# Tuning three places of an attention-plus-MLP kernel: the last output block in two parts, one group's key decay on another engine, and fewer load issues in one stretch

## The chip, the cores and the metric

The kernel runs on one core of a Trainium2 chip. The metric is the device time of one execution in microseconds (us). The kernel before took 225.02 us (median of 3 runs, 224.54 to 225.32).

## The reference

A block-wise linear attention with a decay per head, whose output feeds a two-layer MLP with a Mish gate:

```python
# q, k, v: (4 batches, 8 heads, 768 tokens, 64); lam: one decay per head; block = 64
for b in range(nb):
    intra = einsum('bhic,bhjc->bhij', qb, kb) * Dmask      # lam ** (i - j), lower triangle
    intra = einsum('bhij,bhjd->bhid', intra, vb)
    inter = einsum('bhid,bhde->bhie', qb * lam_pow, kv_state)
    out[:, :, sl] = intra + inter
    kv_state = lam_block * kv_state + einsum('bhsd,bhse->bhde', kb * rev_pow, vb)
x = out.transpose(0, 2, 1, 3).reshape(3072, 512)
h = x @ w_in                                               # 512 x 2048
return (h * tanh(softplus(h))) @ w_out                     # Mish; 2048 x 512
```

## The kernel before

The 768 tokens are cut into six groups (n = 0 to 5) of 128 tokens in each of the four batches; i = 4n + b numbers one batch of one group. While TensorE does the MLP of group n (16 units `ph` of the first layer, then 16 quarter-units `po` of the second), the attention of group n + 1 is slipped in between in small pieces. The queues: GpSimd issues the loads (they convert to 16 bits; only the first two of k and `lam` come through SP), SyncE (SP) the transposes, ScalarE (ACT) the outputs.

```python
    def scale_k(i):                                   # the decay of k
        t = work.tile([128, H, D], F16, name="ktil", tag="ktil", bufs=6)
        (nc.vector if i <= B else nc.gpsimd).tensor_tensor(
            out=t, in0=kn[i], in1=bc(lk, 2, D), op=ALU.mult)
        ktil[i] = t

    def turn(i):                                      # decay, then q and k transposed by DMA
        scale_k(i)
        for src, name, to in ((qn, "qraw", qraw), (ktil, "kraw", kraw)):
            to[i] = work.tile([128, JP, C], F16, name=name, tag=name, bufs=4)
            nc.sync.dma_start_transpose(out=to[i], in_=src[i].rearrange("p h c -> p (h c)"))

    ahead = [                                         # the loads of the third group
        (lambda f=f, i=i: f(i)) for i in range(2 * B, 3 * B) for f in (load_k, load_q, load_v)
    ]

    def att_a(s):                                     # first piece of one half (hf) of one batch
        ...
        if n >= NT:                                   # groups 2 to 5: k and q come transposed
            ...
            if hf == 0 and i + 2 < s.loaded:
                turn(i + 2)
            ...
            return
        ...                                           # groups 0 and 1: transposed on TensorE (pk, pq)
        if n > 0:
            if hf == 0 and i + 1 < s.loaded:
                scale_k(i + 1)
            elif hf == 0:
                turn(i + 1)
            att_w(s)                                  # state update; raw on VectorE, w on GpSimd
            ahead.pop(0)()                            # one load issue in each half

    def mm2_unit(n, b, part):
        w = NKI // WS
        if part == 0:
            po_t[0] = ps.tile([128, DMO], F32, name="po", tag="po", bufs=2)
        po = po_t[0]
        for kk in range(w):
            ...                                       # nc.tensor.matmul(po, hsg[n]..., wout[part]...)
        if part == WS - 1:
            osb = work.tile([128, DMO], F32, name="osb", tag="osb", bufs=3)
            nc.scalar.activation(osb, po, AF.Copy)
            r0 = b * S + n * C
            nc.scalar.dma_start(out=out[r0 : r0 + C, :], in_=osb)
```

The names used below: `ktil` is the decayed k, `pk` its transpose by TensorE, `kraw` its transpose by DMA; `raw` and `w` carry the attention's state, `sb` its masked scores; `hsg` is the Mish of `ph`; `osb` is the copy of the result `po` out of PSUM (TensorE's output memory), which the output DMA sends. A DMA lands when its completion is reported.

In the unit loop of group n, `turn((n + 1) * B)` and `turn((n + 1) * B + 1)` are called after the first `ph` unit (for n > 1); what is left in `ahead` is issued after the loop of n = 0.

## Time and profile before

| | before |
|---|---|
| span of the profiled run | 223.3 us |
| TensorE (PE) busy | 210.9 us, 94% |
| VectorE / ScalarE / GpSimd busy | 48% / 48% / 51% |
| PE's waits for GpSimd's `ktil`, 43 to 52 us | 0.37 + 0.54 + 0.58 us |
| PE's wait for `hsg`, 159.3 to 160.6 us | 1.29 us |
| last matmul's end to the end of the span | 4.4 us |

The page's first lines give the span and each engine's busy time; the rows of digits cut the span into 40 slices and give the busy share of each in tenths. In the views PE is TensorE, PEld its weight loads, DVE VectorE, ACT ScalarE and POOL GpSimd; a q after the name (ACTq) marks what the engine's instruction queue does, such as sending off a DMA.

```profile
span 223.3 us, 3697 instructions
...
PE 210.9 (94%) x1413; PEld 112.4 (50%) x1413; DVE 106.4 (48%) x223; ACT 106.8 (48%) x211; POOL 112.9 (51%) x139
...
PE   7697999998999999999999999999799999999992
```

TensorE is busy nearly all the time after the first four slices (22 us); only its gaps can be won. The view of waits, for PE alone, says who ended them (total us, times, longest us):

```profile
PE ph L343 <- ACT hsg L355: 1.8, 2, 1.3
PE pk L254 <- POOL ktil L181: 1.5, 3, 0.6
```

The first gap is in the second group's attention. In the timeline a row is start, duration, engine, line, operation, with idle time and releaser in brackets. PE's rows of the three waits, and the first `ph` after that stretch:

```profile
43.38 0.28 PE L254 MATMUL pk<-ident,ktil 128*128 128x128 f16 x2 [0.37 <-POOL ktil L181]
...
47.60 0.28 PE L254 MATMUL pk<-ident,ktil 128*128 128x128 f16 x2 [0.54 <-POOL ktil L181]
...
51.87 0.28 PE L254 MATMUL pk<-ident,ktil 128*128 128x128 f16 x2 [0.58 <-POOL ktil L181]
...
58.08 1.24 PE L343 MATMUL ph<-xt,win_77 128*128 128x512 f16 x5
```

GpSimd's rows of one batch in the same timeline show why: one decay, two `w`, two load issues, back to back, 4.27 us from one `ktil` to the next (50.76 - 46.49).

```profile
46.49 1.05 POOL L181 TENSOR_TENSOR ktil<-kn,lk 128x512 f16<-128x512 f16 x1
...
47.50 0.73 POOL L220 TENSOR_TENSOR w_200<-raw,lbm 128x256 f16<-128x256 f32 x1
...
48.17 0.94 POOL L77 DMA_DIRECT2D vz_69<-in_v_dram  x1
...
49.13 0.74 POOL L220 TENSOR_TENSOR w_202<-raw,lbm 128x256 f16<-128x256 f32 x1
...
49.80 0.94 POOL L70 DMA_DIRECT2D kn<-in_k_dram  x1
...
50.76 1.05 POOL L181 TENSOR_TENSOR ktil<-kn,lk 128x512 f16<-128x512 f16 x1
```

The second gap is at 159.3 us. The chain of waits, in order of time (start, length, what), runs back from PE through a Mish on ScalarE and an output DMA's issue to the landing of a transpose that has nothing to do with either:

```profile
155.18 4.32 DMA kraw<-ktil
159.49 0.02 issue
159.52 0.02 ACTq L374
...
159.57 0.35 ACTq L374
159.92 0.05 issue
159.97 0.60 ACT hsg L355
160.57 0.04 issue
160.61 6.20 PE ph L343 x28
```

ScalarE's timeline of the same moment: `osb` was ready at 157.63 + 0.60 = 158.23, the DMA that sends it went out at 159.57.

```profile
157.63 0.60 ACT L372 ACTIVATE osb<-po 128x512 f32<-128x512 f32 x1 [1.34 <-PE po L366]
159.57 0.35 ACTq L374 DMA_DIRECT2D out_dram<-osb  x1
```

Meanwhile four decays run on GpSimd, and a VectorE multiply that takes 0.41 to 0.58 us in 29 of its 32 uses takes 3.31 (the other two long ones, 1.50 and 1.32 us at 88.7 and 121.0 us, also ran beside decays on GpSimd):

```profile
154.07 4.26 POOL L181 TENSOR_TENSOR ktil<-kn,lk 128x512 f16<-128x512 f16 x4
154.12 3.31 DVE L239 TENSOR_TENSOR qT<-qraw,lq 128x256 f16<-128x256 f16 x1
```

The third gap is the tail. After these rows only the landing and the closing of the program follow, up to 223.3:

```profile
217.87 1.03 PE L366 MATMUL po<-wout_84,hsg 128*128 128x512 f16 x4
...
218.93 0.60 ACT L372 ACTIVATE osb<-po 128x512 f32<-128x512 f32 x1 [2.86 <-PE po L366]
219.56 0.34 ACTq L374 DMA_DIRECT2D out_dram<-osb  x1
```

### The profile page before, as it was taken

What the parts mean: (1) busy time and instruction counts of PE and PEld (TensorE: products, weight loads), DVE (VectorE), ACT (ScalarE), POOL (GpSimd) and SP (SyncE); (2) the same over time, 40 slices, a digit from 0 to 9 for tenths busy, and PEclk for the clock granted to TensorE, in tenths of its full rate; (3) what the DMA queues carried; (4) which work ended last, traced back from release to release, by engine and by line L of the source; (5) the groups of instructions that cost most, each with busy time, mean ns of one, the idle gap of its engine ahead of it and who ended that gap; (6) DMA issues with size and microseconds to landing.
All of it is one profiled execution on the core that took longest, in us unless ns stands there. A gap on an engine that the chain in (4) does not pass through costs nothing.

```text
span 223.3 us, 3697 instructions
## 1 busy us (share of the span) xinstructions
PE 210.9 (94%) x1413; PEld 112.4 (50%) x1413; DVE 106.4 (48%) x223; ACT 106.8 (48%) x211; POOL 112.9 (51%) x139
## 2 busy tenths in 40 slices
PE   7697999998999999999999999999799999999992
PEld 2374544565445555445555455555345555444440
DVE  7794411566409996249965059956405342000000
ACT  5984662566566322566332566323375323566121
POOL 7993344999947888339869038869300000000000
PEclk9999999999999999999999999999999999999999
DMA  6999999999994999919998919999940012100121
GB/s 108 142 152 207 204 206 171 183 143 137 146 139 50 127 141 146 199 24 105 100 152 98 182 29 114 116 154 82 190 80 0 0 65 79 47 0 3 47 94 49
DMA packets 100130, 24.62 MB, mean 110 GB/s; under 512 B 92945, under 2 KB 97041, under 8 KB 100113
## 3 DMA queue, kind: packets, MB, share of 16 engines
q0 software_dynamic: 77024, 13.37, 76.6%
q1 hardware_dynamic: 19632, 4.73, 14.5%
q10 hardware_dynamic: 3456, 6.29, 8.5%
q8 instruction: 11, 0.18, 0.3%
q14 instruction: 7, 0.05, 0.1%
HBM read 27.27 MB, written 6.29 MB: 150 GB/s over the span
## 4 chain that ended last, share of the span: by engine, by line
PE 72%; DMA 12%; POOL 11%; issue 2%; ACT 1%; DVE 0%; POOLq 0%; ACTq 0%
PE po L366 31%; PE ph L343 30%; DMA wout_84<-in_moe_w_out_dram 9%; PE pS L280 3%; PE pO L302 3%; POOL qn L74 2%; DMA kraw<-ktil 2%; POOL kn L70 2%; PE pO L298 2%; PE pv L205 1%; POOL ktil L181 1%; DMA out_dram<-osb 1%; POOL vz_69 L77 1%; ACT osb L372 1%; POOL vz_70 L77 0%
## 5 line engine op out<-in xcount | busy, mean ns | idle before, releaser
L355 ACT ACTIVATE hsg<-ph 128x512 f16<-128x512 f32 x96 | 57.1, 597 | 33.0 <-PE ph L343 30.8
L366 PEld LDWEIGHTS <-hsg 128*128 128x128 f16 x384 | 34.8, 98 | 30.3 <-issue 0.7
L284 DVE TENSOR_TENSOR sb<-pS,maskT 128x512 f16<-128x512 f32 x48 | 32.9, 685 | 26.7 <-PE pS L280 26.4
L372 ACT ACTIVATE osb<-po 128x512 f32<-128x512 f32 x24 | 14.3, 597 | 40.6 <-PE po L366 40.6
L305 ACT ACTIVATE xt<-pO 128x256 f16<-128x256 f32 x48 | 18.3, 382 | 30.7 <-PE pO L302 28.3
L74 POOL DMA_DIRECT2D qn<-in_q_dram x24 | 21.7, 906 | 7.0 <-DMA win_78<-in_moe_w_in_dram 2.9
L343 PE MATMUL ph<-xt,win_77 128*128 128x512 f16 (+2 forms) x104 | 22.8, 362 | 2.5 <-ACT hsg L355 1.8
L366 PE MATMUL po<-wout_84,hsg 128*128 128x512 f16 x96 | 24.6, 379 | 0.4 <-DMA wout_84<-in_moe_w_out_dram 0.4
L366 PE MATMUL po<-wout_82,hsg 128*128 128x512 f16 x96 | 24.6, 379 | 0.0
L366 PE MATMUL po<-wout_81,hsg 128*128 128x512 f16 x96 | 24.6, 379 | 0.0
L366 PE MATMUL po<-wout_83,hsg 128*128 128x512 f16 x96 | 24.6, 379 | 0.0
L343 PE MATMUL ph<-xt,win_79 128*128 128x512 f16 x96 | 23.3, 379 | 0.0
L343 PE MATMUL ph<-xt,win_80 128*128 128x512 f16 x96 | 23.3, 379 | 0.0
L70 POOL DMA_DIRECT2D kn<-in_k_dram x22 | 20.5, 934 | 4.9 <-DMA wout_83<-in_moe_w_out_dram 1.7
L343 PE MATMUL ph<-xt,win_78 128*128 128x512 f16 x96 | 22.3, 379 | 0.0
L239 DVE TENSOR_TENSOR qT<-qraw,lq 128x256 f16<-128x256 f16 x32 | 20.5, 641 | 0.0
L181 POOL TENSOR_TENSOR ktil<-kn,lk 128x512 f16<-128x512 f16 x19 | 20.5, 1097 | 0.1
L343 PEld LDWEIGHTS <-win_77 128*128 128x128 f16 x104 | 9.7, 97 | 13.8 <-issue 3.2
L343 PEld LDWEIGHTS <-win_78 128*128 128x128 f16 x96 | 9.1, 98 | 9.9
L343 PEld LDWEIGHTS <-win_80 128*128 128x128 f16 x96 | 8.8, 98 | 7.8
L343 PEld LDWEIGHTS <-win_79 128*128 128x128 f16 x96 | 8.8, 98 | 7.8
L243 DVE COPY kz_151<-kraw 64x256 f16<-64x256 f16 x16 | 5.6, 352 | 13.1 <-DMA kraw<-ktil 12.8
(172 smaller groups left out, 263.3 us busy)
## 6 DMA issues: line engine op xcount, KB each, us to landing
out_dram<-osb ACTq DMA_DIRECT2D x24, 256.0 KB, 2.9
qn<-in_q_dram POOLq DMA_DIRECT2D x24, 128.0 KB, 4.8
kn<-in_k_dram POOLq DMA_DIRECT2D x22, 128.0 KB, 4.5
win_77<-in_moe_w_in_dram POOLq DMA_DIRECT2D x1, 512.0 KB, 7.3
win_78<-in_moe_w_in_dram POOLq DMA_DIRECT2D x1, 512.0 KB, 10.0
win_79<-in_moe_w_in_dram POOLq DMA_DIRECT2D x1, 512.0 KB, 11.8
win_80<-in_moe_w_in_dram POOLq DMA_DIRECT2D x1, 512.0 KB, 13.6
wout_81<-in_moe_w_out_dram POOLq DMA_DIRECT2D x1, 512.0 KB, 15.4
```

What stands on the lines that cost most here:

```text
L70: nc.gpsimd.dma_start(out=kn[i], in_=chunk_rows(k, i))
L74: nc.gpsimd.dma_start(out=qn[i], in_=chunk_rows(q, i))
L181: (nc.vector if i <= B else nc.gpsimd).tensor_tensor(out=t, in0=kn[i], in1=bc(lk, 2, D), op=ALU.mult)
L239: nc.vector.tensor_tensor(out=s.qT, in0=qraw[i][:, 2 * hf : 2 * hf + 2, :], in1=lqh, op=ALU.mult)
L280: nc.tensor.matmul(psS[:, 2 * p + hp, :], s.kz[:, p, hp, :], s.qT[:, p, :], start=True, stop=True,)
L284: nc.vector.tensor_tensor(out=s.sb, in0=psS, in1=bc(maskT, 1, 4), op=ALU.mult)
L302: nc.tensor.matmul(psO[:, p, :], vf[:, o : o + 128], s.sb[:, 2 * p + hp, :], start=(n == 0 and hp == 0), stop=(hp == 1))
L305: nc.scalar.activation(dst, psO, AF.Copy)
L343: nc.tensor.matmul(ph_t[ni][:, lo:hi], win[ni // w][:, kc, (ni % w) * 128 : (ni % w) * 128 + 128], xt[n][:, kc, lo:hi], start=(kc == 0), s ...
L355: nc.scalar.activation(hsg[n][:, ni, :], ph_t.pop(ni), AF.Mish)
L366: nc.tensor.matmul(po, hsg[n][:, ki, b * C : (b + 1) * C], wout[part][:, kk, :], start=(ki == 0), stop=(ki == NKI - 1),)
L372: nc.scalar.activation(osb, po, AF.Copy)
```

## The change

The intent: send most of the last output while the last matmuls still run; take four decays from GpSimd just where they precede the last group's transposes; and thin GpSimd's load issues in the stretch where TensorE waits for it. (The diff is complete but for the old body of `mm2_unit`, shown above.)

```diff
     def scale_k(i):
-        (nc.vector if i <= B else nc.gpsimd).tensor_tensor(
+        (nc.vector if i <= B or i >= (NG - 1) * B else nc.gpsimd).tensor_tensor(
...
             att_w(s)
-            ahead.pop(0)()
+            if hf == 1:
+                ahead.pop(0)()
...
+    def mm2_part(n, b, po, parts, lo, hi):
+        w = NKI // WS
+        for part in parts:
+            for kk in range(w):
+                ki = part * w + kk
+                nc.tensor.matmul(
+                    po[:, lo:hi], hsg[n][:, ki, b * C : (b + 1) * C], wout[part][:, kk, lo:hi],
+                    start=(ki == 0), stop=(ki == NKI - 1),
+                )
+
+    def mm2_out(n, b, po, lo, hi, copy, queue):
+        osb = work.tile([128, hi - lo], F32, name="osb", tag=f"osb{hi - lo}", bufs=3)
+        copy(osb, po[:, lo:hi])
+        r0 = b * S + n * C
+        queue.dma_start(out=out[r0 : r0 + C, lo:hi], in_=osb)
+
+    def act_copy(o, i):
+        nc.scalar.activation(o, i, AF.Copy)
+
     def mm2_unit(n, b, part):
         if part == 0:
             po_t[0] = ps.tile([128, DMO], F32, name="po", tag="po", bufs=2)
         po = po_t[0]
+        if n == NG - 1 and b == B - 1:
+            if part == 0:
+                cut = DMO - 128
+                mm2_part(n, b, po, range(WS), 0, cut)
+                mm2_out(n, b, po, 0, cut, act_copy, nc.scalar)
+                pl = ps.tile([128, DMO], F32, name="po", tag="po", bufs=2)
+                mm2_part(n, b, pl, range(WS), cut, DMO)
+                mm2_out(n, b, pl, cut, DMO, nc.vector.tensor_copy, nc.sync)
+            return
+        mm2_part(n, b, po, (part,), 0, DMO)
         if part == WS - 1:
+            mm2_out(n, b, po, 0, DMO, act_copy, nc.scalar)
```

More of the change, by code (lines that the diff above doesn't have):

```diff
@@ L357 @@
     po_t = [None]
+    def mm2_part(n, b, po, parts, lo, hi):
[14 more added lines that the diff above has]
+        nc.scalar.activation(o, i, AF.Copy)
     def mm2_unit(n, b, part):
-        w = NKI // WS
         if part == 0:
@@ L363, in mm2_unit @@
         po = po_t[0]
-        for kk in range(w):
-            ki = part * w + kk
-            nc.tensor.matmul(
-                po, hsg[n][:, ki, b * C : (b + 1) * C], wout[part][:, kk, :],
-                start=(ki == 0), stop=(ki == NKI - 1),
-            )
+        if n == NG - 1 and b == B - 1:
[8 more added lines that the diff above has]
+        mm2_part(n, b, po, (part,), 0, DMO)
         if part == WS - 1:
-            osb = work.tile([128, DMO], F32, name="osb", tag="osb", bufs=3)
-            nc.scalar.activation(osb, po, AF.Copy)
-            r0 = b * S + n * C
-            nc.scalar.dma_start(out=out[r0 : r0 + C, :], in_=osb)
+            mm2_out(n, b, po, 0, DMO, act_copy, nc.scalar)
     scale_k(0)
```

## The prediction

> **What bounds the kernel now.** TensorE: busy 210.9 of 223.3 us (the page, part 1), and 10.00 of every 10 us from 60 to 150 us and from 170 to 210 us (busy time by stretch). So only its 12.4 us of gaps can be won. The waits of PE and the timeline place those that matter here:
> 1. 43 to 53 us, second group's attention: PE waits three times for `ktil` from GpSimd, 0.37 + 0.54 + 0.58 = 1.5 us. GpSimd is 9.9 of 10 us busy there; per batch it does two load issues (0.94 each), one `ktil` (1.05) and two `w` (0.73): 4.4 us, while TensorE needs about 3.6 us.
> 2. 159.3 to 160.6 us: one wait of 1.29 us for `hsg`. The chain of waits goes back: hsg <- the ACT queue's out DMA, issued at 159.57 although `osb` was ready at 158.23 <- landing of the transpose kraw<-ktil (issued 155.18, landed 159.49) <- ktil on GpSimd. The built program of the kernel before explains it: hardware-queue DMAs take eight completion semaphores in turn, and this out DMA is the eighth after that transpose, so it waits for it and holds up the Mish behind it on ScalarE.
> 3. The tail: last matmul ends at 218.9; copy 0.60, landing about 2.85, closing about 0.85: 4.4 us.
>
> **What the change does.**
> - Fewer loads (gap 1). GpSimd's batch falls to 3.5 us, below TensorE's 3.6. The first stall (0.37, behind loads that still come first) stays; the other two should go: -1.1 us. The moved loads make GpSimd issue eight in a row after the group, 7 us, so ktil of the next group's second batch comes at about 63 us, as before (62.75); its use on VectorE is at about 70 us. No new wait.
> - Decay on VectorE (gap 2). 0.68 us instead of 1.07 each, but the first cannot start before the mask multiply that ends at 154.2, so the first transpose starts only about 0.25 us earlier. The larger effect is order: the third and fourth decays now follow VectorE's copies of the first batch, so at least one transpose falls behind the out DMA, which then reuses a semaphore of a DMA that landed long ago. -1.3 us if so, -0.25 if not; taken -1.2. It also ends the 3.31 us (normally 0.41) that a `qT` multiply took beside the four GpSimd multiplies, which agrees with the Trainium skill, "SBUF — State Buffer", Who interferes with whom (a VectorE instruction with two SBUF inputs blocks against a GpSimd one that reads SBUF); nothing on TensorE waits for that, so it is worth nothing by itself.
> - Tail (gap 3). TensorE time is equal: 16 x (162 + 54) ns against 16 x 216. The 384-column copy (about 0.49, between 0.38 for 256 and 0.60 for 512) runs under the last 16 matmuls (0.89); after the last matmul there is a VectorE copy of 128 columns (about 0.28, from 0.41 and 0.68 for 256 and 512) and a 64 KB landing (2.0, the shortest out landing seen). -1.0 us. Two queues give no more bandwidth; the gain is in the smaller last piece.
>
> **Prediction.** 225.0 - 1.1 - 1.2 - 1.0 = 221.7 us; 220.7 to 223.3. Faster by over 2%: 0.08; within 2%: 0.90; slower: 0.02.
>
> **What would show it.** PE waits for ktil fall from 1.5 to about 0.4; the second group's first `ph` starts near 57.1 (58.25); the ACT out DMA follows its osb at once in the fourth group and the 1.29 us PE wait is gone; from last matmul to end 3.4 us.
>
> **What would make it wrong.** The out DMA still waits for a transpose, or the new order ties another DMA to a late one; the eight-load burst delays the third group's kraw; the small last DMA takes as long as the 256 KB one.

## The result, and the profile after

The changed kernel took 221.68 us (median of 4 runs, 221.08 to 222.44), against 224.82 us for the kernel before (median of 4). The ratio is 0.986, with a 95% interval of 0.982 to 0.990. Ratios are the mean time of one kernel's runs over that of the other's of the same rounds, so not quite the ratio of the medians quoted. Executions in which one die ran at a lower clock are left out of the means. With more runs of both it was 0.9836 (221.16 against 224.86 us). The prediction was 221.7 us.

The lines of the changed kernel's page that answer to those of before (line numbers are shifted by the added code):

```profile
span 220.7 us, 3725 instructions
...
PE 210.8 (96%) x1429; PEld 113.7 (52%) x1429; DVE 105.2 (48%) x228; ACT 106.9 (48%) x211; POOL 108.5 (49%) x135
```

TensorE's busy time is the same to 0.1 us; what went is gaps. Its waits for the same two releasers:

```profile
PE ph L344 <- ACT hsg L356: 0.5, 1, 0.5
PE pk L254 <- POOL ktil L181: 0.4, 1, 0.4
```

The remaining 0.5 is near 30 us and was there before; the 1.3 is gone. Of the three waits for `ktil` only the first is left, and the stretch from that `pk` to the next group's first `ph` is 57.85 - 44.33 = 13.52 us instead of 58.08 - 43.38 = 14.70:

```profile
44.33 0.28 PE L254 MATMUL pk<-ident,ktil 128*128 128x128 f16 x2 [0.38 <-POOL ktil L181]
...
57.85 1.46 PE L344 MATMUL ph<-xt,win_77 128*128 128x512 f16 x6
```

GpSimd's timeline: from one `ktil` to the next 49.83 - 46.51 = 3.32 us, with one load issue in place of two. TensorE, whose `pk` of two batches are 3.52 us apart (47.85 - 44.33), is now the slower of the two.

```profile
46.51 1.06 POOL L181 TENSOR_TENSOR ktil<-kn,lk 128x512 f16<-128x512 f16 x1
47.52 0.73 POOL L220 TENSOR_TENSOR w_200<-raw,lbm 128x256 f16<-128x256 f32 x1
48.20 0.73 POOL L220 TENSOR_TENSOR w_202<-raw,lbm 128x256 f16<-128x256 f32 x1
48.87 0.94 POOL L74 DMA_DIRECT2D qn<-in_q_dram  x1
49.83 1.06 POOL L181 TENSOR_TENSOR ktil<-kn,lk 128x512 f16<-128x512 f16 x1
```

In ScalarE's timeline the output DMA follows its `osb` within 0.03 us, and the two Mish follow at once:

```profile
157.43 0.60 ACT L377 ACTIVATE osb<-po 128x512 f32<-128x512 f32 x1 [1.34 <-PE po L365]
158.06 0.34 ACTq L374 DMA_DIRECT2D out_dram<-osb  x1
158.44 1.31 ACT L356 ACTIVATE hsg<-ph 128x512 f16<-128x512 f32 x2 [0.42 <-PE ph L344]
```

VectorE's timeline there: two decays in 1.28 us, and `qT` in 0.42.

```profile
153.91 1.28 DVE L181 TENSOR_TENSOR ktil<-kn,lk 128x512 f16<-128x512 f16 x2
155.11 0.42 DVE L239 TENSOR_TENSOR qT<-qraw,lq 128x256 f16<-128x256 f16 x1
```

And the tail, PE, ScalarE, VectorE and SP together. The first part (384 columns) is copied and sent while the last 16 matmuls run:

```profile
216.56 0.49 ACT L377 ACTIVATE osb<-po 128x384 f32<-128x384 f32 x1 [2.00 <-PE po L365]
...
217.03 0.39 PE L365 MATMUL po<-wout_84,hsg 128*128 128x128 f16 x4
217.08 0.34 ACTq L374 DMA_DIRECT2D out_dram<-osb  x1
217.46 0.29 DVE L372 COPY osb<-po 128x128 f32<-128x128 f32 x1 [31.23 <-PE po L365]
217.77 0.35 SPq L374 DMA_DIRECT2D out_dram<-osb  x1
```

From the last matmul's end (217.42) to the end of the span (220.66) it is 3.2 us instead of 4.4.

One thing to read with care: the spans differ by 2.6 us (223.3 - 220.7), the times by 3.1. The first 43 us hold nothing that the change touches, but their length varies from run to run, because the weights land earlier or later (PE's wait for `win` near 20 us was between 0 and 2.2 us in the runs below): the second batch's `pk` in the second group came at 43.38 us before and at 44.33 after, and between 41.98 and 44.99 in all the profiled runs below. A sum over the stages does not have this noise.

### The profile page after: what moved, and what is told of

It is laid out like the page before. It is cut to its first block, busy times and chain, and to the rows that moved or that the text cites. A ratio compares the mean times of both kernels' runs of the same rounds, so it can differ in the third digit from the quotient of the medians.

```text
span 220.7 us, 3725 instructions
## 1 busy us (share of the span) xinstructions
PE 210.8 (96%) x1429; PEld 113.7 (52%) x1429; DVE 105.2 (48%) x228; ACT 106.9 (48%) x211; POOL 108.5 (49%) x135
## 4 chain that ended last, share of the span: by engine, by line
PE 78%; DMA 10%; POOL 9%; issue 1%; ACT 1%; ACTq 0%; DVE 0%; POOLq 0%
PE po L365 34%; PE ph L344 32%; DMA wout_84<-in_moe_w_out_dram 10%; PE pO L303 4%; PE pS L281 4%; POOL qn L74 2%; PE pO L299 2%; PE pv L205 1%; POOL kn L70 1%; POOL ktil L181 0%; PE pk L254 0%; POOL vz_70 L77 0%; POOL vz_71 L77 0%; POOL vz_72 L77 0%; POOL vz_76 L77 0%
## 5 line engine op out<-in xcount | busy, mean ns | idle before, releaser
L365 PEld LDWEIGHTS <-hsg 128*128 128x128 f16 x400 | 35.8, 98 | 29.8 <-issue 0.8
L377 ACT ACTIVATE osb<-po 128x512 f32<-128x512 f32 (+1 forms) x24 | 14.2, 593 | 39.9 <-PE po L365 39.9
L365 PE MATMUL po<-wout_84,hsg 128*128 128x512 f16 (+2 forms) x100 | 24.8, 370 | 0.6 <-DMA wout_84<-in_moe_w_out_dram 0.6
L365 PE MATMUL po<-wout_81,hsg 128*128 128x512 f16 (+2 forms) x100 | 24.8, 370 | 0.0
L365 PE MATMUL po<-wout_82,hsg 128*128 128x512 f16 (+2 forms) x100 | 24.8, 370 | 0.0
L365 PE MATMUL po<-wout_83,hsg 128*128 128x512 f16 (+2 forms) x100 | 24.8, 370 | 0.0
L239 DVE TENSOR_TENSOR qT<-qraw,lq 128x256 f16<-128x256 f16 x32 | 17.5, 547 | 0.4 <-DMA qraw<-qn 0.4
L181 POOL TENSOR_TENSOR ktil<-kn,lk 128x512 f16<-128x512 f16 x15 | 16.2, 1092 | 0.1
```

The lines of the kernel that those rows point to most:

```text
L181: (nc.vector if i <= B or i >= (NG - 1) * B else nc.gpsimd).tensor_tensor(out=t, in0=kn[i], in1=bc(lk, 2, D), op=ALU.mult)
L239: nc.vector.tensor_tensor(out=s.qT, in0=qraw[i][:, 2 * hf : 2 * hf + 2, :], in1=lqh, op=ALU.mult)
L365: nc.tensor.matmul(po[:, lo:hi], hsg[n][:, ki, b * C : (b + 1) * C], wout[part][:, kk, lo:hi], start=(ki == 0), stop=(ki == NKI - 1),)
L377: nc.scalar.activation(o, i, AF.Copy)
```

## The experiments

All outputs are right. The stages are read from PE's timeline and the end of the span: A is from the second batch's first `pk` of the second group to the first `ph` after it; B from that `ph` to the last matmul's end; L from there to the last landing of an output, and Z from that landing to the end of the span. The times are medians of 6 runs (4 for the change's first call); the "before" medians of the calls are 224.96, 225.27, 224.86 and 224.66 (225.2 and 224.6 in the two that hold a slow run, without it).

| run | time, us | ratio to before | A | B | L | Z |
|---|---|---|---|---|---|---|
| before | 224.82 | 1 | 14.71 | 160.81 | 2.71 | 1.66 |
| changed | 221.68 | 0.986 | 13.53 | 159.56 | 1.96 | 1.29 |
| loads_only | 224.25 | 0.9967 | 13.52 | 160.51 | 2.70 | 1.67 |
| decay_only | 223.31 | 0.9921 | 14.72 | 159.50 | 2.71 | 1.69 |
| tail_only | 223.61 | 0.9942 | 14.72 | 160.95 | 1.97 | 1.15 |
| before_tiny1 | 223.79 | 0.994 | 14.56 | 159.69 | 2.69 | 1.19 |
| after_tiny2 | 222.2 | 0.9868 | 13.52 | 160.89 | 1.97 | 1.03 |
| tail_one_queue | 221.62 | 0.985 | 13.53 | 159.54 | 1.95 | 1.63 |
| tail_parallel | 221.35 | 0.9844 | 13.63 | 159.50 | 2.65 | 1.22 |
| tail_parallel2 | 221.89 | 0.9884 | 13.52 | 160.28 | 2.44 | 1.34 |
| after_again | 221.16 | 0.9836 | 13.53 | 159.54 | 1.97 | 1.28 |
| after_ktil5 | 221.04 | 0.9816 | 13.80 | 159.54 | 1.96 | 1.28 |
| ktil5_again | 221.52 | 0.9835 | 13.98 | 159.54 | 1.97 | 1.29 |
| after_ktil567 | 222.15 | 0.9863 | 14.42 | 159.55 | 1.96 | 1.29 |

Each stage is read from one profiled execution per run. Where its code is the same, L repeats to 0.02 us, A to 0.16, and B to 0.06 where no output waits; with the wait B lies between 160.51 and 160.95. Z varies by 0.66 us for a reason told below. The times vary by some tenths and more, so the verdicts below rest on the stages A, B and L; the 95% intervals of the ratios are about 0.003 wide to each side.

### Each part alone

`loads_only` is the kernel before with the second hunk of the diff, `decay_only` with the first, `tail_only` with the rest.

```diff
# loads_only
             att_w(s)
-            ahead.pop(0)()
+            if hf == 1:
+                ahead.pop(0)()
# decay_only
-        (nc.vector if i <= B else nc.gpsimd).tensor_tensor(
+        (nc.vector if i <= B or i >= (NG - 1) * B else nc.gpsimd).tensor_tensor(
```

> Only the fewer load issues. My theory: of TensorE's three waits for ktil in the second group's attention (0.37, 0.54, 0.58 us before) the last two go, so the stretch from the first L266 eviction to the first matmul of the second group's mm1 is 1.1 to 1.2 us shorter; the 1.29 us wait for hsg near 160 us and the tail of 4.4 us stay as before. Time about 1.1 us below before (ratio 0.995). Rival (the eight-load burst costs as much as it saves): a new wait of about 1 us shows on TensorE between 65 and 75 us, or the third group's start is no earlier, and the ratio is 1.000.

Measured: 0.9967 (0.9934 to 1.0001). Stage A is 1.19 us shorter, one wait for `ktil` of 0.6 us is left, and B keeps the `hsg` wait (1.0 us in this run). PE has no wait at all between 60 and 80 us, so the burst of eight load issues costs TensorE nothing.

> Only the last group's decay on VectorE. My theory (order of the completion semaphores): in the program as built the out DMA is now the 49th hardware-queue DMA and follows the 41st, an earlier out DMA, instead of 50th after the 42nd, the transpose kraw<-ktil; it is issued within 0.05 us of its osb, TensorE's 1.29 us wait for hsg is gone, and kraw lands only 0.2 to 0.4 us earlier. Rival (the decay itself was late): kraw lands over 1 us earlier, and the out DMA still is issued at that landing. Rival 2 (the shared port: VectorE was held 3.3 us by GpSimd): the gain comes from VectorE's earlier operations, and some TensorE wait for VectorE near 157 to 161 us disappears. All of them: about 1.2 us below before (ratio 0.9945); the first and the third differ in what the trace shows.

Measured: 0.9921 (0.9889 to 0.9952). A is unchanged and B is 1.31 us shorter. The output DMA went out at 158.08, 0.02 us after its `osb` (157.46 + 0.60). The transpose was issued at 154.65, against 155.18 before, in a run in which everything there came 0.17 us earlier (the mask multiply before it at 153.34 against 153.51); so it started about 0.4 us sooner. It landed at 158.78 against 159.49, about 0.5 us sooner: more than the 0.2 to 0.4 expected, but not the rival's 1, and the output had left 0.7 us before that landing.

> Only the last output in two column parts. Theory: from the last matmul's end to the end of the span 3.3 us instead of 4.4; the rest as before, with the 1.29 us wait for hsg still there. Time 1.1 us below before (ratio 0.995). If the three single parts add up to the whole change (3.1 to 3.6 us), their gains are independent.

Measured: 0.9942 (0.9907 to 0.9977). L and Z together are 3.12 us instead of 4.37; B still has the 1.3 us wait. The three savings in these runs, 1.19 + 1.31 + 1.25 = 3.75 us, and those of the whole change against before, 1.18 + 1.25 + 1.12 = 3.55 us, agree to 0.2 us, most of which is Z: within that the parts are independent.

### Why the decay helps: order, not speed

The program as built numbers the hardware-queue DMAs (those of SP and ScalarE) and gives them eight completion semaphores in turn. A DMA waits until the previous user of its semaphore has landed. From the built programs, around the output of the fourth group's last batch (number 50 before, 49 after; "batch 1" is the first batch of the last group):

```
before:  42 kraw (batch 1)  43 out  44 qraw  45 kraw  46 qraw  47 kraw  48 qraw  49 kraw  50 out
after :  41 out  42 out  43 kraw (batch 1)  44 qraw  45 kraw  46 qraw  47 kraw  48 qraw  49 out  50 kraw
```

Before, output number 50 shares a semaphore with 42, the transpose that lands at 159.5. After, the last `kraw` has moved behind the output, the output is number 49, and its partner 41 is an output that landed long before. To separate this from the two rivals (the decay came sooner; VectorE was freed from GpSimd), one load that nobody needs was put into the kernel before:

```diff
                 turn((n + 1) * B + 1)
+                if n == NG - 2:
+                    nc.sync.dma_start(out=idle[:, 0:H], in_=lam.unsqueeze(0))
```

(The small tile `idle` is made further up.)

> The kernel before plus one idle load of 32 bytes on the SP queue after the second transpose pair of the last group, with the decay still on GpSimd. It does no useful work; it only moves the out DMA by one place, so it takes the semaphore after the previous out DMA (which in the trace of before landed at 153.91 + 4.9 = 158.8) instead of after the transpose (landed 159.5). Theory of the order: the out DMA is issued at the previous out DMA's landing, about 158.8 instead of 159.57, TensorE's wait for hsg shrinks from 1.29 to about 0.5 to 0.7 us, and qT still takes 3.3 us beside GpSimd. Both rivals (late decay, shared port): nothing moves, the wait stays 1.3 us, the time is that of before or 0.1 us longer.

Measured: 0.994 (0.9904 to 0.9975): an added, useless load made the kernel faster. ScalarE's timeline of `before_tiny1`:

```profile
159.10 0.60 ACT L372 ACTIVATE osb<-po 128x512 f32<-128x512 f32 x1 [1.34 <-PE po L366]
159.89 0.36 ACTq L374 DMA_DIRECT2D out_dram<-osb  x1
```

The DMA went out 0.19 us after `osb` (159.89 - 159.70) instead of 1.34 us after it, with the decay still on GpSimd and `qT` still at 3.31 us. B is 159.69, that is 1.12 us shorter. (Z is shorter too, by 0.47 us, for the reason told under "The closing", so the ratio alone would say too much.) The expectation was a smaller gain, because in the trace of before the previous output landed 0.6 us after `osb`; in this run it landed at 159.82, 0.12 us after it.

The reverse: the changed kernel with two such loads, which bring output and transpose back onto one semaphore (numbers 51 and 43).

```diff
                 turn((n + 1) * B + 1)
+                if n == NG - 2:
+                    for e in range(2):
+                        nc.sync.dma_start(out=idle[:, e * H : (e + 1) * H], in_=lam.unsqueeze(0))
```

> The changed kernel plus two idle 32-byte loads on the SP queue after the last group's second transpose pair; the decay stays on VectorE. In the program as built the out DMA is then the 51st and takes the semaphore of the 43rd, the transpose kraw<-ktil, again. Theory of the order: the out DMA is issued at that transpose's landing (about 4.4 us after its issue, 0.9 to 1.0 us after osb was ready), TensorE waits 0.9 to 1.0 us for hsg, although VectorE does the decay and qT takes 0.42 us; about 1 us of the gain is lost (some 2.3 us below before, ratio 0.990). Rivals (the decay came sooner, or the shared port was freed): no wait returns, time as the changed kernel (ratio 0.986).

Measured: the wait is back, and larger than expected: the output left 1.37 us after its `osb`, and TensorE waited 1.3 us. B is 160.89, as before the change, though VectorE does the decays and `qT` is short. ScalarE's timeline of `after_tiny2`:

```profile
156.58 0.60 ACT L377 ACTIVATE osb<-po 128x512 f32<-128x512 f32 x1 [1.34 <-PE po L365]
158.55 0.34 ACTq L374 DMA_DIRECT2D out_dram<-osb  x1
158.94 1.09 ACT L356 ACTIVATE hsg<-ph 128x512 f16<-128x512 f32 x2 [1.76 <-DMA kraw<-ktil]
```

The transpose was issued at 153.78 and landed 4.7 us later, at 158.5. The ratio, 0.9868, lies above that of `after_again` (0.9836), but their intervals overlap, so the total alone would not have decided; the stage does. Both rivals fall. The moment agrees too: in all five profiles in which this output waits (before, loads_only, tail_only, before_tiny1, after_tiny2) it left 0.08 us after the landing of the DMA eight places before it, a transpose in four of them and an output in before_tiny1.

### The tail: two engines, or an early first part

```diff
# tail_one_queue
-                mm2_out(n, b, pl, cut, DMO, nc.vector.tensor_copy, nc.sync)
+                mm2_out(n, b, pl, cut, DMO, act_copy, nc.scalar)
```

> The changed kernel with the last 128 columns also copied by ScalarE and sent from ScalarE's queue. Theory (the gain is in the smaller last piece): the first copy and its issue end about 0.05 us before the last matmul's result is there, so the second copy starts at most 0.1 us later, and from the last matmul to the end of the span it is 3.3 to 3.4 us, as with two engines and queues. Rival (two engines and queues matter): at least 0.3 us longer, 3.6 us or more.

Measured: the second copy (0.28 us on ScalarE, 0.29 on VectorE) began when the last matmul ended, and L is 1.95 us, as with two engines (1.96). The sum L + Z, 3.58 us, is above the 3.3 to 3.4 that was expected and just under the rival's 3.6, but the excess is all in Z, the closing, which is told below. Up to the landing, the second engine and queue bring nothing. The 0.75 us of L are the last piece's own: its copy took 0.29 us instead of 0.60, and its landing 1.60 instead of 2.04. This agrees with the Trainium skill, "Trainium Kernel Development and Optimization", Key Constraints: DMAs of several queues run on the same DMA engines, and issuing from several engines only saves issue time.

```diff
# tail_parallel: both halves after the last matmul, columns 0-255 and 256-511 of one tile
-                cut = DMO - 128
-                mm2_part(n, b, po, range(WS), 0, cut)
+                cut = DMO // 2
+                mm2_part(n, b, po, range(WS), 0, DMO)
                 mm2_out(n, b, po, 0, cut, act_copy, nc.scalar)
-                pl = ps.tile([128, DMO], F32, name="po", tag="po", bufs=2)
-                mm2_part(n, b, pl, range(WS), cut, DMO)
-                mm2_out(n, b, pl, cut, DMO, nc.vector.tensor_copy, nc.sync)
+                mm2_out(n, b, po, cut, DMO, nc.vector.tensor_copy, nc.sync)
```

> The changed kernel, but the last 16 matmuls write all 512 columns as before, and afterwards ScalarE copies columns 0 to 255 and VectorE 256 to 511 at the same time, each sending 128 KB on its own queue. Two engines and two queues, but no part leaves early. Theory (the small late piece matters, not the second queue): copies 0.38 and about 0.41 us, landing between that of 64 KB (1.6) and of 256 KB, so from the last matmul to the end 3.6 to 3.9 us, 0.3 to 0.6 us longer than the changed kernel. Rival (the second engine and queue bring the gain): 3.3 us, as the changed kernel.

Measured: L + Z is 3.87 us, within the expectation, but not for its reason. VectorE's copy began at 217.19, when ScalarE's had ended (its idle time is put down to `ACT osb`), so the two did not run at the same time and L is 2.65, hardly below the 2.71 of one piece. It did not test what it should. The last run gave each half a PSUM tile of its own and interleaved the matmuls:

```diff
# tail_parallel2
+                pl = ps.tile([128, DMO], F32, name="po", tag="po", bufs=2)
+                for ki in range(NKI):
+                    for t, lo in ((po, 0), (pl, cut)):
+                        nc.tensor.matmul(t[:, lo:lo + cut], ...)   # 256 columns each
+                mm2_out(n, b, po, 0, cut, act_copy, nc.scalar)
+                mm2_out(n, b, pl, cut, DMO, nc.vector.tensor_copy, nc.sync)
```

> As tail_parallel, whose two copies ran one after the other (VectorE's began when ScalarE's had ended), but with the two halves in two PSUM tiles, their matmuls interleaved so that both are complete only at the end; the copies should now start together. No part leaves early. Theory (an early first part and a small late one): from the last matmul to the landing of the later half 2.2 to 2.35 us (0.42 copy, 1.8 landing), between the 2.72 of one 256 KB piece and the 2.05 of the changed kernel: two engines at once give about 0.4 of the 0.67 us, the early departure the rest. Rival (all of it is the second engine and queue): 2.05 or less. If the copies still wait for each other: 2.7.

Measured: the copies overlapped (215.71 and 215.82), and L is 2.44 us, slightly outside the 2.2 to 2.35 expected, because the landing of the later half took 1.95 us and not 1.8. So two engines at once bring 0.27 of the 0.75 us of the changed kernel; sending the first part early, with a small second part, brings all 0.75 even on one engine (an early first part and a small last one come together here; no run parts them). The version pays elsewhere: TensorE needs both tiles at once and waits 0.6 us for an older output's eviction (B is 160.28). By the stages it is slower than the change (B 0.7 and L 0.5 us longer); the intervals of the ratios overlap.

**The closing.** After the last landing SP checks the eight completion semaphores one after the other. In the trace, checks that need not wait are 0.06 to 0.10 us apart, but in most runs one of them comes 0.46 to 0.49 us late. In before, loads_only, decay_only and tail_one_queue that pause falls after the last landing, and Z is 1.63 to 1.69 us; in before_tiny1 there is none, in tail_only and after_tiny2 it comes before the last landing, and in the changed kernel and the other versions that send the last piece from SP it coincides with the wait for it: Z is 1.03 to 1.34. So about 0.4 us of the tail's saving (1.66 - 1.29) is not from the smaller piece but from where this pause falls.

The raw traces narrow the cause. In 13 of the 14 profiles the pause stands before the same instruction of SP, the 80th that the trace holds, whichever check that is; 0.63 to 0.69 us after that instruction an 8 KB transfer of the kind `instruction` starts on DMA queue 14. In before_tiny1, which has one SP instruction more, the 80th comes at the end of a 3.4 us wait for an earlier output, and the transfer starts 1.1 us into that wait: the pause is hidden there. So its place is set by the number of SP's instructions, and tail_one_queue, which has two fewer than the changed kernel, pays 0.34 us in Z (1.63 against 1.29). That the pause is the fetching of SP's instructions fits this, but no run tested it.

### Can the last wait for ktil go too?

```diff
# after_ktil5 (ktil5_again is the same kernel)
-        (nc.vector if i <= B or i >= (NG - 1) * B else nc.gpsimd)
+        (nc.vector if i <= B + 1 or i >= (NG - 1) * B else nc.gpsimd)
# after_ktil567
+        (nc.vector if i < 2 * B or i >= (NG - 1) * B else nc.gpsimd)
```

> The changed kernel with one more decay, that of the second group's second batch, on VectorE. It should take away the one wait for ktil that is left (0.38 us): from the first pk of the second group to the first ph of its mm1 16.2 to 16.4 us, against 17.86 before and 16.68 in the changed kernel. Total about 0.4 us below the changed kernel, 3.6 us below before (ratio 0.984). If VectorE becomes the limit there, no gain or up to 0.3 us worse.

Measured: 0.9816 (0.9786 to 0.9845), the lowest of all; no wait for GpSimd's `ktil` is left; from the first `pk` to the first `ph` it is 57.04 - 40.62 = 16.42 us, just outside the expectation. It is no gain either: tail_one_queue, the same as the changed kernel up to the tail, has 16.43 us there with the decay still on GpSimd, since the wait for `ktil` did not come in that run. Both kernels were run again together:

> The changed kernel once more, beside the two others of this call, so that they are compared on one chip and with one set of runs of before: ratio 0.986, 3.1 us below before.

> The changed kernel with the decay of the second group's second batch on VectorE too, once more. In earlier runs the wait for ktil that it removes varied from 0 to 1.0 us with the landing of the weights. Ratio 0.983, 0.4 to 0.7 us below the changed kernel of the same call; TensorE waits for no ktil of GpSimd.

Measured: 0.9836 (0.9807 to 0.9864) and 0.9835 (0.9805 to 0.9866); no difference. In `after_again` TensorE's weight load waited 1.2 us for `ktil` at this place (PE's own wait there, 0.7 us, is put down to an `osb` on ScalarE that came last). In `ktil5_again` that wait is gone, but PE waits 0.2 us for the landing of a `v` load and 0.3 us for VectorE's `sb`, and stage A is 13.98 us instead of 13.53. From the first `pk` to the first `ph` it is 16.98 us (56.81 - 39.83) and 16.94 us (56.95 - 40.01). Taking one wait away let the next ones show. No version shown here beats the changed kernel with certainty.

> The changed kernel with all the second group's decays on VectorE. GpSimd loses 3 x 1.07 us more, VectorE gains 3 x 0.69. The ktil waits are gone as with one, so the same stretch is again 16.2 to 16.4 us; what might be lost is that each decay stands before raw and the mask multiply on VectorE, 0.7 us later per batch: if TensorE then waits for sb, the stretch is 16.5 us or more. GpSimd's ktil of the third group's second batch comes about 2 us earlier (near 61.5), which is worth nothing on TensorE. Ratio 0.984 to 0.986.

Measured: a miss for the main expectation, and the stated loss came true. The stretch is 57.68 - 40.64 = 17.04 us. VectorE's decays stand ahead of the mask multiply, and TensorE now waits for that more often; PE's waits in `after_ktil567` and, for comparison, in `after_ktil5`:

```profile
PE pS L281 <- DVE sb L285: 1.1, 5, 0.3
```

```profile
PE pS L281 <- DVE sb L285: 0.4, 2, 0.2
```

GpSimd's later `ktil` came at 63.05, not near 61.5 as expected: GpSimd waited for VectorE's `raw` instead.

## Why the prediction was right or wrong

- *Total 221.7 us, 220.7 to 223.3; within 2%.* Right: 221.68 us, and 221.16 later. That it is met to 0.02 us is luck: the stages saved 3.55 us where 3.3 were forecast.
- *Fewer loads, -1.1 us; the first stall stays, the other two go; no new wait.* Right: A is 1.18 us shorter in the whole and 1.19 alone. The sign given for it, the second group's first `ph` near 57.1 us, did not come (57.85), because that run reached the stretch 0.95 us later; counted from its start it did. That the first stall is a constant 0.37 us was too simple: in the profiled runs with GpSimd's decay it was between 0 and 1.0 us; what sets it was not tested.
- *Decay on VectorE: -1.3 us if the order changes, -0.25 if not.* Right in mechanism and size: B is 1.25 to 1.31 us shorter, and the two runs with idle loads took the wait away without the decay and brought it back in spite of it.
- *The 3.31 us `qT` is a port conflict that TensorE does not feel.* The part on the path is shown: `before_tiny1` kept the 3.31 us and had 1.12 of the 1.3 us. That VectorE is held by GpSimd's multiplies agrees with the Trainium skill, "SBUF — State Buffer", Who interferes with whom, and with the 0.42 us after the decays left GpSimd; no run changed only the port.
- *Tail -1.0 us.* The sum was about right (1.12), its terms were not, and that their errors cancel is luck. The prediction put the 256 KB landing at 2.85 and the closing at 0.85 us; measured are 2.05 (219.56 to 221.61) and 1.66. (2.85 is near the median of all output landings on the page, 2.9; the last three of the run took 2.0.) The 64 KB landing was put at 2.0 and took 1.6. So the shorter path to the landing brought 0.75 us, and a shift in the closing, which the prediction did not have, 0.4. "Two queues give no more bandwidth; the gain is in the smaller last piece" held up to the landing, not for the closing.

## What to carry to other kernels

A kernel whose main engine is busy nearly all the time gains only at that engine's gaps, so price each part of a change by the gap that it closes and by nothing else. When an instruction starts at the very moment at which an unrelated DMA lands, look at the order in which the built program hands out completion semaphores: a different order, even one useless DMA more, can be worth over 1 us. Send the last output in an early large and a late small part, and keep the stages apart when you measure, since the total may vary by more than the change is worth.

## What the Trainium skill lacked or had wrong

- "DMA: Bandwidth & Descriptors", Why a DMA increments its semaphore by 16 and not by 1, says why DMAs in flight need semaphores of their own; no page that I read says what the cure costs when a few are reused in turn by all hardware queues: here an output waited 1.34 us for an unrelated transpose and TensorE 1.29 us behind it, and moving it by one place in the order took away 1.12 us.
- "DMA: Bandwidth & Descriptors", Rules for kernel authors, advises to coalesce because small transfers pay mostly overhead. The runs agree about the overhead (64 KB from SP landed in 1.6 us, 256 KB in 2.05), but for the last output the split was still right: 0.75 us earlier, because the first part left before the last matmul's end and only 64 KB were left to copy and send.
- No page that I read tells of a pause in the closing checks of the semaphores on SP: one check comes 0.46 to 0.49 us late, in most runs, and the end of the program moves with it (1.03 to 1.69 us after the last landing). It stands before the 80th instruction of SP, 0.63 to 0.69 us before an 8 KB `instruction` transfer; the cause is not tested.
